# An attention and mixer kernel: the channel products' operands become scaled float16 pairs

## The chip, the core and the metric

The kernel runs on one core of a Trainium2 chip. Its engines work from queues of their own: TensorE (PE, with its weight loads shown apart as PEld), VectorE (DVE), ScalarE (ACT), GpSimd (POOL) and SyncE (SP), which issues the DMAs. The metric is the device time of one execution in microseconds (us); a kernel's time is the median of several runs. The profile is one execution recorded by the hardware.

## The reference

Eight batches, eight heads, 576 positions, 64 columns a head. Attention is masked by blocks of 64; its output, laid side by side over the heads (512 channels), goes through a mixer with four weights.

```python
scores = q @ k.T / sqrt(64), masked to block_i >= block_j
attn = softmax(scores);  x = (attn @ v), heads side by side     # per batch 576 x 512
theta = x @ w_theta
zr, zi = x * cos(theta), x * sin(theta)
y = w_tok_r @ zr + w_tok_i @ zi                                 # over positions
u = x + y
out = u + max(u @ w_ch, 0)                                      # over channels
```

## The kernel before

The work is cut into some 2570 named parts: loads, one evicting step, one group of products and so on. The order of all parts is written out by hand: the list `PLACES` (from line 32) gives each part a place, `BANKS` the bank of the matmul memory for each group, `ON` (line 185) the engine of each part that several engines could do (P, D, A for GpSimd, VectorE, ScalarE), and `RUNNING` (line 181) places at which fillers, products of ones, keep TensorE at work; there are 49 of them. Each engine's queue holds its parts in that order.

A pair is two heads of one batch; there are 32. For a pair the scores are products (L554, L567), a maximum of each row is taken on VectorE (L588), the exponentials on ScalarE (L592). For the first four pairs the exponentials are turned by TensorE (L604) and evicted by VectorE or ScalarE (`keep_half`, L611 and L613); for the others they are split into two float16 parts (`high` on ScalarE, `low` on VectorE, L619) and turned by a DMA. Products with the values (L638) and a normalising step (L653) give one tile of x per pair, kept in `x_ring`, a ring of `X_BUFS = 6` tiles.

The mixer, per batch: x is split into two float16 parts and turned; the angles are products with `wth_h` and `wth_l` (`theta`, L727), brought to turns (L737, L743) and through sine and cosine on ScalarE (L749 to L763). `times_x` (L773) makes z, in ten pieces a batch, on VectorE or GpSimd; `z_high` and `z_low` (L786) split it. The token products (`mix`, L796) take 27 products of 288 columns for each of eight results, three per block of positions: high times high, low times high, high times low. `add_parts` (L801) puts x into `u_all`, `unscale` (L805) takes the batch's scale off it, `take_u` (L809) adds the token product. For the channel products u is split into `uh` (ScalarE, L815) and `ul` (VectorE or GpSimd, L820), both 32-bit, and `channel` (L828) takes 12 products of 288 columns for each of eight results, with the 32-bit weights `wch_h` and `wch_l`. `rectify` (L834) adds the clipped result to u, and `store` (L838) writes four tiles a batch. `u_all` is one buffer of four tiles: the next batch's sums wait for the stores.

The weights come in 64-bit and are narrowed (`exponent`, `narrow`, L397 to L406). For the token and angle weights `most` (L410) sums the magnitudes, and from these a power of two is made (`w_reduce`, `w_diagonal`, `w_all`, `w_scale`) by which `high_part` (L415) and `low_part` (L421) scale them into two float16 parts. The channel weights have no scale: L417 and L424. The raw weights go in turn through two buffers that are later `uh` and `ul`.

```python
for ww, uu in ((wch_h, uh), (wch_h, ul), (wch_l, uh)):
    nc.tensor.matmul(g[:, 0:HS], lhsT=ww[:, dt, e * P:(e + 1) * P], rhs=uu[:, dt, th * HS:(th + 1) * HS],
                     start=(n == 0), stop=(n == 11))
```

Of the kernel before, what the change touches and what calls it, by code (L numbers as in the profile page):

```python
# [28 lines left out]
X_BUFS = 6  # L29
# [171 lines left out]
      "xs": "DDDDDDDDDDDDDDDD",  # L201
      "xd": "DDDDAAAAAAAAADAD",
      "uh": "AAAAAAAAAAAAAAAA",
      "ul": "DDDPDPPPPPPPDDPP"}
WHOLE = 4
PLAIN = 16

# [878 lines left out]
```

## Time and profile before

| | us |
|---|---|
| median of 3 runs | 680.8 (678.14 to 681.47) |
| profiled execution | 677.4 |
| its span, first to last instruction | 675.6 |
| TensorE busy | 658.2 (97%) |
| VectorE busy | 563.8 (83%) |
| ScalarE busy | 525.9 (78%) |
| GpSimd busy | 186.7 (28%) |
| mean granted TensorE clock | 0.997 |

A share of busy time is an average over the span. The end of a product is modelled, and products overlap, so a busy TensorE says only that one was under way; the pace of products is read from the chain, where each piece lasts until the next begins.

### The profile page before, as it was taken

Reading aid. Unit: us, or ns where it says so; the run is one execution under the profiler, and the core shown is the slowest. Engines: PE = TensorE matmul, PEld = TensorE weight load, DVE = VectorE, ACT = ScalarE, POOL = GpSimd, SP = SyncE. Lnnn points to the kernel's source line nnn. Section 1 sums busy time; section 2 is a strip of 40 time slices with the busy share of each in tenths; the row PEclk is TensorE's granted clock in tenths of the full one; section 3 lists DMA queues with packets and bytes.
Section 4 is the critical chain, followed back from the end, with each engine's and each line's share of the span. In section 5 each row is a group of like instructions: output and inputs, shape, how many; then the busy total and the mean of one; then the engine's idle time right before and its main releaser. Section 6 shows DMA issues by size and latency. Waiting matters only on the chain.

```text
span 675.6 us, 17319 instructions
## 1 busy us (share of the span) xinstructions
PE 658.2 (97%) x7263; PEld 530.9 (79%) x7263; DVE 563.8 (83%) x825; ACT 525.9 (78%) x812; POOL 186.7 (28%) x195
## 2 busy tenths in 40 slices
PE   8899999999979999999999999999999999999997
PEld 4688757889658868887798878888788887886887
DVE  4889897988988888999989888989888989864832
ACT  5999898877898699987987789878998689627410
POOL 1432222400042114241362323252054113011611
PEclk9999999999989999999999999999999999999999
DMA  9972357999969995899968896979978962960101
GB/s 337 334 257 79 106 102 137 228 214 182 244 85 229 213 197 128 182 176 207 195 176 181 165 193 147 191 131 186 203 176 181 170 131 60 172 105 1 71 1 71
DMA packets 245854, 110.51 MB, mean 164 GB/s; under 512 B 227216, under 2 KB 227216, under 8 KB 245776
## 3 DMA queue, kind: packets, MB, share of 16 engines
q1 hardware_dynamic: 245776, 109.40, 74.2%
q8 instruction: 57, 0.93, 0.6%
q14 instruction: 21, 0.17, 0.1%
HBM read 43.06 MB, written 9.44 MB: 78 GB/s over the span
## 4 chain that ended last, share of the span: by engine, by line
PE 74%; ACT 10%; DVE 8%; DMA 5%; issue 2%; POOL 0%; SPq 0%; DVEq 0%; ACTq 0%; POOLq 0%
PE ps L796 27%; PE ps L828 15%; PE ps L727 11%; PE ps L638 10%; PE ps L554 9%; DMA pt<-p 3%; ACT t L592 2%; DVE m L588 2%; DVE p L619 1%; PE ps L567 1%; DMA w_raw<-in_w_tok 1%; DMA k<-in_kT 1%; ACT aa L761 1%; DVE v L540 1%; ACT p L316 1%
## 5 line engine op out<-in xcount | busy, mean ns | idle before, releaser
L592 ACT ACTIVATE t<-ps,m 128x320 f32<-128x320 f32 (+4 forms) x320 | 149.3, 528 | 40.3 <-DVE m L588 31.7
L796 PE MATMUL ps<-wT_h,zl 128*128 128x288 f16 x540 | 155.1, 287 | 0.9 <-POOL zl L786 0.9
L796 PE MATMUL ps<-wT_h,zh 128*128 128x288 f16 x540 | 155.3, 288 | 0.4 <-ACT zh L314 0.4
L796 PE MATMUL ps<-wT_l,zh 128*128 128x288 f16 x540 | 155.0, 287 | 0.0
L588 DVE TENSOR_REDUCE m<-ps 128x2 f32<-128x128 f32 (+4 forms) x160 | 125.4, 817 | 21.9 <-PE ps L559 15.4
L796 PEld LDWEIGHTS <-zh 128*128 128x128 f16 x1080 | 106.0, 98 | 28.6 <-ACT zh L314 0.9
L638 PE MATMUL ps<-v,pt 128*128 128x65 f16 (+1 forms) x2760 | 114.5, 200 | 2.6 <-DVE x_ring L653 2.4
L619 DVE SCALAR_TENSOR_TENSOR p<-t,p 128x1664 f16<-128x1664 f32 x56 | 107.9, 1929 | 8.2 <-ACT p L316 8.0
L316 ACT ACTIVATE p<-t 128x1664 f16<-128x1664 f32 x56 | 88.8, 1591 | 6.5 <-DMA pt<-p 5.4
L638 PEld LDWEIGHTS <-pt 128*128 128x128 f16 x2520 | 82.2, 97 | 9.0 <-issue 4.8
L727 PE MATMUL ps<-wth_h,xt 128*128 128x512 f16 (+1 forms) x384 | 87.6, 345 | 0.5 <-DVE xt L713 0.3
L727 PEld LDWEIGHTS <-xt 128*128 128x128 f16 (+1 forms) x576 | 46.0, 102 | 44.3 <-issue 2.2
L828 PE MATMUL ps<-uh,wch_h 128*128 128x288 f32 x256 | 79.5, 310 | 0.0
L828 PE MATMUL ps<-ul,wch_h 128*128 128x288 f32 x256 | 75.7, 296 | 0.0
L828 PE MATMUL ps<-uh,wch_l 128*128 128x288 f32 x256 | 75.6, 295 | 0.0
L796 PEld LDWEIGHTS <-zl 128*128 128x128 f16 x540 | 53.1, 98 | 13.8 <-POOL zl L786 1.1
L727 PE MATMUL ps<-wth_l,xt 128*128 128x512 f16 (+1 forms) x192 | 57.3, 344 | 0.0
L554 PE MATMUL ps<-k,qh 64*128 64x288 f32 (+3 forms) x384 | 51.2, 400 | 2.7 <-ACT pt L611 1.5
L786 POOL TENSOR_TENSOR zl<-aa,zh 128x512 f16<-128x512 f32 (+1 forms) x27 | 33.7, 1255 | 71.1 <-ACT zh L314 71.1
L828 PEld LDWEIGHTS ps<-uh,wch_h 128*128 128x128 f32 x256 | 48.1, 188 | 2.8 <-issue 1.2
L809 DVE SCALAR_TENSOR_TENSOR u_all<-ps,sizes,u_all 128x288 f32<-128x288 f32 x64 | 31.8, 512 | 20.2 <-PE ps L796 19.2
L828 PEld LDWEIGHTS ps<-ul,wch_h 128*128 128x128 f32 x256 | 48.1, 188 | 0.3
(141 smaller groups left out, 1214.1 us busy)
## 6 DMA issues: line engine op xcount, KB each, us to landing
raw_v<-in_v SPq DMA_DIRECT2D x32, 384.0 KB, 4.3
q<-in_qT SPq DMA_DIRECT2D x32, 320.0 KB, 3.8
k<-in_kT SPq DMA_DIRECT2D x32, 320.0 KB, 3.6
out<-u_all SPq DMA_DIRECT2D x32, 288.0 KB, 2.4
w_raw<-in_w_tok SPq DMA_DIRECT2D x9, 576.0 KB, 5.8
w_raw<-in_w_theta SPq DMA_DIRECT2D x4, 512.0 KB, 7.6
w_raw<-in_w_ch SPq DMA_DIRECT2D x4, 512.0 KB, 4.9
pt<-p SPq DMA_TRANSPOSE x56, 6.4
```

Of the source, the lines that this page charges most:

```text
L316: engine.mul(to, x, scale)
L540: nc.vector.scalar_tensor_tensor(out=self.v2[:, :, :, 0:D], in0=self.v, scalar=self.batch.up, in1=self.v1[:, :, :, 0:D], op0=ALU.mult, op1 ...
L554: nc.tensor.matmul(s[hh][:, col:col + n], lhsT=qq[rows, i * P:(i + 1) * P], rhs=kk[rows, k0:k0 + n], start=nn == 0 and (j == 0 or c == "ab ...
L588: nc.vector.tensor_reduce(out=m, in_=s, axis=AX.XY if i in (2, 3) else AX.X, op=ALU.max, negate=True)
L592: nc.scalar.activation(out=to, in_=s, func=AF.Exp, scale=1.0, bias=m)
L619: nc.vector.scalar_tensor_tensor(out=self.p[:, 1, :], in0=self.t, scalar=LIFT, in1=self.p[:, 0, :], op0=ALU.mult, op1=ALU.subtract)
L638: nc.tensor.matmul(o[:, i, :], lhsT=pp[:, block, :], rhs=vv[:, of, hh, :], start=nn == 0, stop=nn == n - 1)
L727: nc.tensor.matmul(g[rows, 0:cols.stop - cols.start], lhsT=x[:, dt, part, i, rows], rhs=ww[:, dt, cols], start=(n == 0), stop=(n == 11))
L786: engine_of("zl", (2 * self.b + hf) * 5 + n).tensor_tensor(out=zl, in0=cv, in1=zh, op=ALU.subtract)
L796: nc.tensor.matmul(g, lhsT=zz[:, kk, cols], rhs=ww[:, kk, ts], start=(n == 0 and kk == k0 and nn == 0), stop=(n == 4 and nn == 2))
L809: nc.vector.scalar_tensor_tensor(out=self.u(dt)[:, ts], in0=bank("y", self.b, dt, th)[:, 0:HS], scalar=self.batch.unit, in1=self.u(dt)[:, ...
L828: nc.tensor.matmul(g[:, 0:HS], lhsT=ww[:, dt, e * P:(e + 1) * P], rhs=uu[:, dt, th * HS:(th + 1) * HS], start=(n == 0), stop=(n == 11))
```

## The change

The channel products' operands become scaled float16 pairs, as the token products' are. For that the channel weights get a sum of magnitudes and a scale of their own, and u is kept in a scaled form throughout: `unscale` multiplies x by a factor for all batches (`g_x`) in place of the batch's own, `take_u` uses `g_y`, and a new step `unlift` (parts "fin") multiplies the result by `unit` before the store, one of 576 columns a tile, two of 288 in the last batch. The factors come from `gains`, eight small steps, which need a bound on the token product: `sums_of_tok`, 18 products of ones with the magnitudes of the token weights, made before their high parts are written. `uh` is f16(u x scale), on ScalarE; `ul` is always on VectorE. Both share one buffer, `uhl`. The freed space holds `u_all` twice, for even and odd batches, and eight tiles in `x_ring`. The raw weights go in turn through `uhl` and through `p_both`, the two tiles of split exponentials now in one. `PLACES`, `BANKS`, `RUNNING` (52 fillers) and `ON` are new; in `ON`, z has 35 pieces on VectorE (46 before), its low parts 33 (30), evictions of turned exponentials 7 (5), scalings of the first values 3 (1), and "fin" has 40, of which 36 are used: 12 on GpSimd, 11 on VectorE, 13 on ScalarE.

```diff
-X_BUFS = 6
+X_BUFS = 8
-    (12, 0, 7), (24, 0, 12), (33, 0, 3), (46, 0, 4), (65, 0, 2), (75, 0, 2), (314, 0, 2), (371, 3, 10), (386, 5,
-    2), (740, 1, 5)
+    (12, 0, 7), (25, 0, 13), (43, 0, 8), (63, 0, 3), (75, 0, 3), (336, 0, 3), (396, 3, 8), (404, 5, 2), (767, 1, 5)
...
-    u_all = const.tile([P, NDT, S], F32, name="u_all")
+    u_all = [const.tile([P, NDT, S], F32, name=f"u{i}") for i in range(2)]
-    p_parts = [const.tile([P, 2, WIDE], F16, name=f"p{i}") for i in range(2)]
+    p_both = const.tile([P, 2 * 2 * WIDE], F16, name="p")
+    p_parts = [p_both.rearrange("p (h a c) -> p h a c", h=2, a=2)[:, hh] for hh in range(2)]
-    wch_h = const.tile([P, NDT, DM], F32R, name="wch_h")
-    wch_l = const.tile([P, NDT, DM], F32R, name="wch_l")
+    wch_h = const.tile([P, NDT, DM], F16, name="wch_h")
+    wch_l = const.tile([P, NDT, DM], F16, name="wch_l")
-    raws = [mo.tile([P, 2, 2 * S], U32, tag=tag, name="w_raw") for tag in ("uh", "ul")]
+    raws = [mo.tile([P, 2, 2 * S], U32, tag="uhl", name="w_raw"),
+            p_both[:, 0:8 * S].bitcast(U32).rearrange("p (k c) -> p k c", k=2)]
...
         def high_part(self):
-            if self.kind in w_up:
-                times(engine_of("w5", self.unit), self.hi, self.val, w_up[self.kind])
-            else:
-                nc.scalar.copy(out=self.hi, in_=self.val)
+            times(engine_of("w5", self.unit), self.hi, self.val, w_up[self.kind])
         def low_part(self):
-            if self.kind in w_up:
-                nc.vector.scalar_tensor_tensor(out=self.lo, in0=self.val, scalar=w_up[self.kind], in1=self.hi, op0=ALU.mult,
-                                               op1=ALU.subtract)
-            else:
-                nc.gpsimd.tensor_tensor(out=self.lo, in0=self.val, in1=self.hi.bitcast(F32), op=ALU.subtract)
+            nc.vector.scalar_tensor_tensor(out=self.lo, in0=self.val, scalar=w_up[self.kind], in1=self.hi, op0=ALU.mult,
+                                           op1=ALU.subtract)
+    def sums_of_tok():
+        g = bank("w1")
+        for th in range(2):
+            for kt in range(NK):
+                nc.tensor.matmul(g[:, th * BANK:th * BANK + HS], lhsT=ones, rhs=wT_h[:, kt, th * HS:(th + 1) * HS].bitcast(BF16),
+                                 start=kt == 0, stop=kt == NK - 1)
...
         def u_parts(self):
-            return [self.tile_of(tag, [P, NDT, S], F32R) for tag in ("uh", "ul")]
+            both = self.tile_of("uhl", [P, 2, NDT, S], F16)
+            return [both[:, i] for i in range(2)]
...
-            times(engine_of("xd", self.b * 2 + dp), u, u, self.batch.down)
+            times(engine_of("xd", self.b * 2 + dp), u, u, g_x)
...
-            engine_of("ul", self.b * 2 + dp).tensor_tensor(out=ul[:, two, ts], in0=u_all[:, two, ts], in1=uh[:, two, ts].bitcast(F32), op=ALU.subtract)
+            nc.vector.scalar_tensor_tensor(out=ul[:, two, ts], in0=u_all[self.b % 2][:, two, ts], scalar=w_down["ch"],
+                                           in1=uh[:, two, ts], op0=ALU.mult, op1=ALU.subtract)
...
+        def unlift(self, e, *th):
+            u = self.u(e)[:, th[0] * HS:(th[0] + 1) * HS] if th else self.u(e)
+            times(engine_of("fin", (self.b * NDT + e) if not th else B * NDT + 2 * e + th[0]), u, u, self.batch.unit)
...
-        if kind != "ch":
-            add(("wa", n), w.most, scaled)
-            scaled += [("wc", kind, 2)]
+        add(("wa", n), w.most, scaled)
+        scaled += [("wc", kind, 2)] + ([("wd",)] if kind == "tok" else [])
...
+    add(("wd",), sums_of_tok, [("wa", n) for n, w in enumerate(todo) if w[0] == "tok"], takes=[(("w1",), 2)])
-            free = turn_of(f"u{dp}", [("store", b, dt) for dt in two])
+            free = turn_of(f"u{dp}", [("store", b, dt) for dt in two], 2)
-            part("store", (e,), m.store, [("out", b, e, th) for th in range(2)])
+            halves = [(th,) for th in range(2)] if b == B - 1 else [()]
+            for th in halves:
+                part("fin", (e,) + th, m.unlift, [("out", b, e, i) for i in th or (0, 1)] + [("us", b, 0)])
+            part("store", (e,), m.store, [("fin", b, e) + th for th in halves])
```

## Rows read from the trace of the kernel before

**Rows 1.** Busy time of each engine, and the chain that ended last by engine.
```profile
PE 658.2 (97%) x7263; PEld 530.9 (79%) x7263; DVE 563.8 (83%) x825; ACT 525.9 (78%) x812; POOL 186.7 (28%) x195
PE 74%; ACT 10%; DVE 8%; DMA 5%; issue 2%; POOL 0%; SPq 0%; DVEq 0%; ACTq 0%; POOLq 0%
```
**Rows 2.** Stretches: start:end, length, busy us (x instructions) per engine, granted clock, DMA.
```profile
17.00:104.40 87.40, 81.23 (x714) 64.78 (x713) 77.85 (x126) 82.36 (x132) 26.89 (x37) 1.00 0.54 173
...
190.00:197.00 7.00, 3.49 (x56) 2.52 (x55) 6.41 (x11) 7.00 (x12) 5.08 (x4) 0.92 0.24 50
197.00:260.00 63.00, 63.00 (x698) 48.25 (x697) 55.62 (x77) 53.01 (x83) 11.72 (x12) 0.98 0.97 195
260.00:350.00 90.00, 89.78 (x1092) 74.50 (x1089) 84.99 (x122) 79.08 (x123) 35.53 (x30) 1.00 0.86 178
...
104.40:575.00 470.60, 466.24 (x5593) 378.74 (x5592) 422.36 (x607) 395.66 (x610) 136.31 (x124) 1.00 0.87 176
```
**Rows 3.** Chain in order of time, before 105 us: start us, us, what.
```profile
39.21 1.36 DVE m L588
...
52.91 2.66 DVE wT_l L421 x2
...
56.40 0.74 DVE pt L613
...
75.46 1.78 ACT t L592 x3
...
99.06 1.90 ACT t L592 x3
```
**Rows 4.** Chain in order of time, near 190 us.
```profile
190.60 1.05 ACT aa L761
```
**Rows 5.** Chain in order of time, from 621 us.
```profile
621.46 11.20 PE ps L828 x84
632.66 26.11 PE ps L796 x213
...
662.39 9.61 PE ps L828 x72
```
**Rows 6.** Weight loads by form: count, busy us, mean ns, idle before.
```profile
L796 PEld LDWEIGHTS <-zl 128*128 128x128 f16 x540 | 53.1, 98 | 13.8 <-POOL zl L786 1.1 <-DVE zl L786 0.4
...
L828 PEld LDWEIGHTS ps<-ul,wch_h 128*128 128x128 f32 x256 | 48.1, 188 | 0.3
```
**Rows 7.** Groups by form or line, work of the first 105 us (L534: min/median/max ns).
```profile
L421 DVE SCALAR_TENSOR_TENSOR wth_l<-w_val,size_theta,wth_h 128x1024 f16<-128x1024 f32 x2 | 2.5, 1280 | 0.0
L410 ACT ACTIVATE wth_h<-w_val 128x1024 f16<-128x1024 f32 x2 | 2.1, 1062 | 0.0
L613 DVE TENSOR_SCALAR pt<-ps 128x1024 f32<-128x1024 f32 x3 | 3.7, 1223 | 1.2 <-PE ps L604 0.7 <-ACT unused L459 0.5
L613 DVE TENSOR_SCALAR pt<-ps 128x640 f32<-128x640 f32 x2 | 1.6, 814 | 0.0
L611 ACT ACTIVATE pt<-ps 128x1024 f32<-128x1024 f32 x5 | 5.0, 1034 | 0.2
L611 ACT ACTIVATE pt<-ps 128x640 f32<-128x640 f32 x6 | 4.3, 710 | 0.0
L588 DVE TENSOR_REDUCE m<-ps 128x2 f32<-128x640 f32 x32 | 26.1, 816 | 0.6 <-PE ps L559 0.6
...
L534 DVE TENSOR_SCALAR v<-raw_v,sizes x1: 609/609/609, 30.4 to 30.4; 128x768 f32<-128x768 f32 x1
```
**Rows 8.** Low part of u, z and scaling: by line (min/median/max ns) or by form.
```profile
L820 DVE TENSOR_TENSOR ul<-u_all,uh x6: 1346/1358/2251, 126.5 to 609.8; 128x1152 fp32r<-128x1152 f32 x6
L820 POOL TENSOR_TENSOR ul<-u_all,uh 128x1152 fp32r<-128x1152 f32 x8 | 21.7, 2717 | 41.9 <-ACT uh L314 41.9
L773 DVE TENSOR_TENSOR aa<-aa,x_ring x28: 415/680/1786, 90.1 to 627.5; 128x512 f32<-128x512 f32 x18, 128x256 f32<-128x256 f32 x10
L320 DVE TENSOR_SCALAR u_all<-u_all,sizes 128x1152 f32<-128x1152 f32 x6 | 4.8, 807 | 0.1
```

More of the change, by code (lines that the diff above doesn't have):

```diff
@@ L28 @@
 QK_BUFS = 2
-X_BUFS = 6
+X_BUFS = 8
 PLACES = [
[132 rows of a table removed]
[135 rows of a table added]
 ]
 BANKS = [
[11 rows of a table removed]
[11 rows of a table added]
 ]
 RUNNING = [
-    (12, 0, 7), (24, 0, 12), (33, 0, 3), (46, 0, 4), (65, 0, 2), (75, 0, 2), (314, 0, 2), (371, 3, 10), (386, 5,
-    2), (740, 1, 5)
-]
-ON = {"w5": "AAAAAAA",
-      "wc": "PPDPDP",
-      "vc": "DPPDDDPDDDPPDDPPDDPPDDPP",
-      "qh": "APPPPAPAAAAAPAPAAAPAPAPPAAPAPAPP",
-      "vf": "PDPP",
-      "cp": "DADAADAAAADDAAAA",
-      "n0": "DDDDDDDDDAADDDDDAADADADADAAAADDDDAAADDDADDDADDDDDAAAAADAADDADDDA",
+    (12, 0, 7), (25, 0, 13), (43, 0, 8), (63, 0, 3), (75, 0, 3), (336, 0, 3), (396, 3, 8), (404, 5, 2), (767, 1, 5)
+]
+ON = {"w5": "AAAAAAAAA",
+      "wc": "PDDDPPPDP",
+      "vc": "DPDPPPPDPDDPPPDPPPPPPPDP",
+      "qh": "APPPPAPPPAPPPAAPAAAAPPPAPAAPPAAA",
+      "vf": "PDDD",
+      "cp": "DDDADDAADAAAADAA",
+      "n0": "DDADDDDDADDAAAAADDDDDDDADADAAAAAADADADDDAAADADADDADDADADDADDADDA",
       "v1": "DDDDAAAAAAAAAAAAAAAAAAAAAAAAAAAA",
       "high": "DDDDDDDDAAAAAAAAAAAAAAAAAAAAAAAAAAAAAAAAAAAAAAAAAAAAAAAAAAAAAAAA",
-      "kh": "DDDDDDDDDDDDDDDDPAAAPPPAPPPPAPPA",
+      "kh": "DDDDDDDDDDDDDDDDPPAPAPAPPAPAPPAA",
       "kl": "DDDDDDDDDDDDDDDDDDDDDDDDDDDDDDDD",
@@ L368, in attention_phase_mixer @@
             + [mo.tile([P, 1, S], F32, tag="rr", name="w_val")],
-            "ch": u_all[:, :, 0:DM]}
-    w_most = {"theta": const.tile([P, NDT // 2], F32, name="most_theta"), "tok": const.tile([P, (NK + 1) // 2], F32, name="most_tok")}
+            "ch": u_all[1][:, :, 0:DM]}
+    w_most = {"theta": const.tile([P, NDT // 2], F32, name="most_theta"), "tok": const.tile([P, (NK + 1) // 2], F32, name="most_tok"),
+              "ch": const.tile([P, NDT // 2], F32, name="most_ch")}
     w_size = {kind: const.tile([P, 5], F32, name=f"size_{kind}") for kind in w_most}
     w_up, w_down = ({kind: size[:, i:i + 1] for kind, size in w_size.items()} for i in (2, 3))
+    gain = const.tile([P, 7], F32, name="gain")
+    g_most, g_exp, g_down, g_up, g_x, g_out, g_y = (gain[:, i:i + 1] for i in range(7))
     class Weight:
@@ L439, in w_scale, with gains @@
         parts = (w_size[kind][:, i:i + 1] for i in range(4))
-        power_of_two(bank("w", kind) if step < 0 else None, *parts, step, 151.0, engine_of("wc", 3 * (kind == "tok") + step - 1) if step > 0 else None)
+        power_of_two(bank("w", kind) if step < 0 else None, *parts, step, 151.0, engine_of("wc", 3 * ("theta", "tok", "ch").index(kind) + step - 1) if step > 0 else None)
+    def sums_of_tok():
[4 more added lines that the diff above has]
+                                 start=kt == 0, stop=kt == NK - 1)
+    def gains(step):
+        one = float(1 << 23)
+        if step == 0:
+            g = bank("w1").rearrange("p (a c) -> p a c", a=2)[:, :, 0:HS]
+            nc.vector.tensor_reduce(out=g_most, in_=g, axis=AX.XY, op=ALU.max)
+        elif step == 1:
+            nc.gpsimd.tensor_scalar(out=g_most, in0=g_most, scalar1=1.02, scalar2=1.02, op0=ALU.mult, op1=ALU.add)
+        elif step == 2:
+            nc.vector.tensor_scalar(out=g_exp.bitcast(I32), in0=g_most.bitcast(I32), scalar1=23, scalar2=None,
+                                    op0=ALU.logical_shift_right)
+        elif step == 3:
+            nc.gpsimd.tensor_scalar(out=g_down.bitcast(I32), in0=g_exp.bitcast(I32), scalar1=-one, scalar2=253.0 * one, op0=ALU.mult,
+                                    op1=ALU.add)
+        elif step == 4:
+            nc.gpsimd.tensor_scalar(out=g_up.bitcast(I32), in0=g_exp.bitcast(I32), scalar1=one, scalar2=one, op0=ALU.mult,
+                                    op1=ALU.add)
+        elif step == 5:
+            nc.gpsimd.tensor_scalar(out=g_x, in0=g_down, scalar1=w_up["ch"], scalar2=1.0, op0=ALU.mult, op1=ALU.mult)
+        elif step == 6:
+            nc.gpsimd.tensor_scalar(out=g_out, in0=g_up, scalar1=w_down["ch"], scalar2=1.0, op0=ALU.mult, op1=ALU.mult)
+        else:
+            nc.gpsimd.tensor_scalar(out=g_y, in0=g_x, scalar1=w_down["tok"], scalar2=1.0, op0=ALU.mult, op1=ALU.mult)
     sizes = const.tile([P, B, 11], F32, name="sizes")
@@ L476, in unit_of @@
             if i == 0:
[L477 removed]
+                nc.gpsimd.tensor_scalar(out=self.unit, in0=self.down, scalar1=g_out, scalar2=1.0,
                                         op0=ALU.mult, op1=ALU.mult)
@@ L804, in unscale @@
             u = self.u_two(dp)
-            times(engine_of("xd", self.b * 2 + dp), u, u, self.batch.down)
+            times(engine_of("xd", self.b * 2 + dp), u, u, g_x)
         def take_u(self, dt, th):
             ts = slice(th * HS, (th + 1) * HS)
-            nc.vector.scalar_tensor_tensor(out=self.u(dt)[:, ts], in0=bank("y", self.b, dt, th)[:, 0:HS], scalar=self.batch.unit,
+            nc.vector.scalar_tensor_tensor(out=self.u(dt)[:, ts], in0=bank("y", self.b, dt, th)[:, 0:HS], scalar=g_y,
                                            in1=self.u(dt)[:, ts], op0=ALU.mult, op1=ALU.add)
@@ L814, in u_high @@
             ts, two = slice(th[0] * HS, (th[0] + 1) * HS) if th else slice(0, S), slice(2 * dp, 2 * dp + 2)
-            times(engine_of("uh", self.b * 2 + dp), self.u_parts()[0][:, two, ts], u_all[:, two, ts])
+            times(engine_of("uh", self.b * 2 + dp), self.u_parts()[0][:, two, ts], u_all[self.b % 2][:, two, ts], w_down["ch"])
         def u_low(self, dp, *th):
@@ L864, in attention_phase_mixer @@
         scaled = [("w", n, 3)]
-        if kind != "ch":
-            add(("wa", n), w.most, scaled)
-            scaled += [("wc", kind, 2)]
+        add(("wa", n), w.most, scaled)
+        scaled += [("wc", kind, 2)] + ([("wd",)] if kind == "tok" else [])
         add(("w", n, 5), w.high_part, scaled)
         add(("w", n, 6), w.low_part, [("w", n, 5)])
-    for kind in ("theta", "tok"):
+    for kind in ("theta", "tok", "ch"):
         add(("wr", kind), step_of(w_reduce, kind), [("wa", n) for n, w in enumerate(todo) if w[0] == kind])
@@ L876, in attention_phase_mixer @@
                 leaves=() if step >= 0 else [("w", kind)])
+    add(("wd",), sums_of_tok, [("wa", n) for n, w in enumerate(todo) if w[0] == "tok"], takes=[(("w1",), 2)])
+    for step in range(8):
+        needs = {0: [("wd",)], 3: [("wg", 2)], 4: [("wg", 2)], 5: [("wg", 3), ("wc", "ch", 2)], 6: [("wg", 4), ("wc", "ch", 3)],
+                 7: [("wg", 5), ("wc", "tok", 3)]}.get(step, [("wg", step - 1)])
+        add(("wg", step), step_of(gains, step), needs, leaves=[("w1",)] if step == 0 else ())
     for tag, last in (("zh", [("wm", "theta")]), ("zl", [("wm", "tok")]), ("aa", w_last["theta"]), ("rr", w_last["tok"]), ("xt0", w_last["tok"]), ("xt1", w_last["tok"]),
-                      ("uh", [("w", n, 3) for n in range(len(todo))]), ("ul", [("w", n, 3) for n in range(len(todo))])):
+                      ("uhl", [("w", n, 3) for n in range(0, len(todo), 2)]), ("p0", [("w", n, 3) for n in range(1, len(todo), 2)]),
+                      ("p1", [("w", n, 3) for n in range(1, len(todo), 2)])):
         turn_of(tag, last)
     for dp in range(NDT // 2):
-        turn_of(f"u{dp}", [w_last["ch"][dp]])
+        turn_of(f"u{dp}", [w_last["ch"][dp]], 2)
     batches = [Batch(b) for b in range(B)]
@@ L900, in attention_phase_mixer @@
         for i, kind in enumerate(("tok", "theta")):
-            add(("us", b, i), step_of(batch.unit_of, i), [("vc", b, 3), ("wc", kind, 3)])
+            add(("us", b, i), step_of(batch.unit_of, i), [("vc", b, 3), ("wg", 6) if i == 0 else ("wc", kind, 3)])
     mixers = [Mixer(b, batches[b]) for b in range(B)]
@@ L1002, in attention_phase_mixer @@
         c_all = [("c", b, e, th) for e, th in mixes]
-        u_free = turn_of("uh", c_all) + turn_of("ul", c_all)
+        u_free = turn_of("uhl", c_all)
         for dp in range(NDT // 2):
             two = (2 * dp, 2 * dp + 1)
-            free = turn_of(f"u{dp}", [("store", b, dt) for dt in two])
+            free = turn_of(f"u{dp}", [("store", b, dt) for dt in two], 2)
             part("xs", (dp,), m.add_parts, [key for dt in two for key in x_done[dt]] + free)
-            part("xd", (dp,), m.unscale, [("xs", b, dp), ("vc", b, 3)])
+            part("xd", (dp,), m.unscale, [("xs", b, dp), ("wg", 5)])
             for dt in two:
@@ L1014, in attention_phase_mixer @@
                         part("mix", (dt, th, n), m.mix, needs, takes=[("y", 2)] if n == 0 else ())
-                    part("u", (dt, th), m.take_u, [("mix", b, dt, th, 4), ("us", b, 0), ("xd", b, dp)], leaves=[("y", 2)])
+                    part("u", (dt, th), m.take_u, [("mix", b, dt, th, 4), ("wg", 7), ("xd", b, dp)], leaves=[("y", 2)])
             for th in [()] if b < B - 1 else [(0,), (1,)]:
```

20 lines of the change are left out of this document (10 added, 10 removed), and 289 rows, old and new, of tables (BANKS, PLACES).

## The prediction

> **What bounds the kernel now.** I read the busy shares first, then the chain of what ended last, then stretches, and only then single groups. TensorE is busy for 97% of the span and the chain runs over it for 74% of its length; VectorE and ScalarE follow at 83% and 78% [rows 1]. The shares are averages, so the stretches decide. From 17 to 104.4 us the token and angle weights are made ready and the first batch waits for them: ScalarE is busy 82.4 of 87.4 us and VectorE 77.9, and TensorE's 81.2 us there include fillers [rows 2]. From 75 to 101 us the chain runs on ScalarE alone [rows 3]. From 104.4 us on TensorE sets the pace: in 260 to 350 us it is busy 89.8 of 90 us, while VectorE is busy 85.0 of those 90 [rows 2]. One hole is left: from 190 to 197 us TensorE is busy only 3.5 of 7 us, because the chain there hangs on the sines of the next batch on ScalarE [rows 4], and the granted clock falls to a mean of 0.92 in that stretch and 0.98 in the next 63 us, so some of it ran at the lower of its two levels (1.2 instead of 2.4 GHz) [rows 2]. So a shorter TensorE instruction is worth its full price from about 104 us on, and added VectorE or ScalarE work costs time mainly before that.
>
> **The channel products.** All 768 keep their shape (128x128 weights, 288 columns); the operands change from 32-bit to float16. The token products have just that shape in float16. In the last 66 us the chain has both kinds back to back: 84 channel products in 11.20 us and 72 in 9.61 us, 133.4 ns each, and 213 token products in 26.11 us, 122.6 ns each [rows 5]. The gap is 10.8 ns, so 768 x 10.8 = **8.3 us** less, 1.04 us for each of eight batches. The weight loads agree: 188 ns against 98 ns [rows 6]; a load of 188 ns is longer than a product of 133 ns, and the next one begins as the last ends. I take the whole 8.3, since every batch's channel products lie after 104 us. Ends: 0 if it isn't the type that costs (a rival below), 8.3 if it is.
> [...]
>
> **Preparing the weights and the gains.** The channel weights now get what the other weights have: a sum of magnitudes (two more on ScalarE, 1.06 us each), a scale, and a scaled low part on VectorE, 2 x 1.28 us, instead of one on GpSimd [rows 7]. Two more evictions of turned exponentials go from ScalarE to VectorE in net (one of 1024 columns and one of 640: 1.22 + 0.81 us there, 1.03 + 0.71 less on ScalarE), two value scalings go from GpSimd to VectorE (0.61 each), and a reduction over 576 columns is new (about 0.75, from 0.82 for 640 columns) [rows 7]. With some five steps of one column (0.9) and what the new order puts on the other side of the first token product (about -1.4), VectorE gets 2.6 + 2.0 + 1.2 + 0.75 + 0.9 - 1.4 = **6.1 us** more before that product, and ScalarE 2.1 - 1.7 + 0.9 (smaller pieces and order) = **1.3 us**. TensorE gets 18 products of 288 columns for the sums of the token weights (18 x 122.6 ns = 2.2 us) and three fillers more (49 to 52); these run where it waits anyway. The same 59 TensorE parts as before stand ahead of the first token product in the new order, plus those sums and the channel weights' spread, so the freed space brings no work forward there. What does it cost? ScalarE's 1.3 us count in full, as the chain is on it. VectorE is idle for 9.6 us of the stretch [rows 2], so its 6.1 us may vanish; I count 0.9, the share of the chain from 17 to 104.4 us that lies on VectorE (12.9 of 87.4 us, 17 pieces between 39 and 57 us [rows 3]). Together **+2.2 us**. Ends: -1.7 (only ScalarE's relief counts) to +9.6 (1.3, 6.1 and the 2.2 of the sums one after the other; the spread of the token weights' scale stands behind these sums in TensorE's queue, and the high parts of the token weights wait for both).
>
> **Steady work moved.** The low part of u goes wholly to VectorE: 14 of about 1.36 us and 4 half ones of 0.7, against 6 of 1.36 before, +13.7 us; GpSimd loses 8 of 2.72 and 4 half ones, 27 us [rows 8]. Eleven of the z products go from VectorE to GpSimd (0.68 us each, -7.5), three more low parts of z come back (+2.1) [rows 8]. New is the last scaling of u before each store, 28 of 576 columns and 8 of 288: 11 of these on VectorE, about 0.43 and 0.25 us from 0.81 for 1152 columns [rows 8], +4.2; 13 on ScalarE (some 7 us), 12 on GpSimd. With the 6.1 above and small ones (-1.4) VectorE gains about 17.2 us, of which the 11 after the first token product fall nearly all between 104.4 and 575 us. There VectorE is busy 422.4 of 470.6 us now [rows 2]; it would be 433.4 of 464.4 (six batches' gain, 6.2, taken off), 93.3%. The stretch from 260 to 350 us shows it at 94.4% with TensorE still full [rows 2], so I cost this at nothing; if that cover is gone, see the second and fourth case. The scaling of u delays a store by one step and with it the release of that u; but u now has two copies, and the next batch fills the other. SyncE's queue holds the store behind it for that step; the loads queued there were issued earlier. In the freed space the sums of x can be written before the last batch's stores have gone, and two batches of normalised tiles fit. I cost this at 0: after 197 us TensorE has no idle time to give [rows 2]; it could only fill the hole at 190 us (third case).
>
> **The end.** After the last product there are now the rectifying step, the scaling of 288 columns on VectorE (0.25 and a handover) and the store: **+0.3 us**; ends 0.2 to 0.6. The low parts of the last batch take 0.7 us on VectorE instead of 1.4 on GpSimd, while 24 products cover them.
>
> **The sum.** -8.3 + 2.2 + 0.3 = **-5.8 us** against the profiled execution of 677.4 us (span 675.6, 1.8 us around it): 671.6. The median of the runs is 680.8, 3.4 above that execution; I carry the difference over: **675.0 us**.
>
> **The rivals.**
> Second case: VectorE and GpSimd block each other. The low part of u on VectorE takes 1.35 us at best and 2.25 at worst, and a z product 0.68 and 1.79 [rows 8]: a collision costs about 1 us. If each of the ten moved low parts meets one, VectorE has 443.4 us of work from 104.4 to 575; at no more than 94.4% busy the stretch lasts 469.7 instead of 470.6. Then -0.9 + 2.2 + 0.3 - 2.1 (batches 6 and 7) = -0.5: **680.3 us**. Against it: GpSimd's work doesn't grow, since what it gains in z products and scalings it loses in low parts.
> The page "SBUF — State Buffer" of the Trainium skill, section "Who interferes with whom", says that a VectorE instruction with two SBUF inputs contends with a GpSimd instruction that reads SBUF and that the loser waits for the whole instruction. The spread of these rows agrees with that rule.
> Third case: the freed space closes the hole. TensorE's idle 3.5 us and the lower clock (0.08 x 7 + 0.02 x 63 = 1.8 us) go, and the start costs nothing: -8.3 - 5.3 + 0.3 = -13.3: **667.5 us**. For it: two batches of normalised tiles and a second u loosen just the waits between batches. Against it: the hole's chain is on ScalarE, which gets no less to do before it, and five fillers still stand at the same point of the order.
> Fourth case, slower: VectorE's idle time doesn't shrink. If the 48.2 us that it now idles from 104.4 to 575 us are waits inside its own order, its 11 us more lengthen the stretch by 11 us and TensorE's gain there is lost: 11 + 2.2 + 0.3 - 2.1 = +11.4: **692 us**. It is slower from about 6 us of that on. Against it: the 94.4% from 260 to 350 us.
> Fifth case: the change of type gives nothing per product: 2.2 + 0.3 = +2.5: **683.3 us**. Against it: the two prices stand side by side in one stretch.
>
> **How the numbers follow.** Forecast 0.50, second case 0.17, third 0.17, fourth 0.12, fifth 0.04. A measurement of this kernel can tell about 0.5% (3.4 us) from no change. Faster: four fifths of the forecast's half (it may end 2.4 us higher), the third case, and a little of the second, 0.62. Slower: the fourth, 0.12. The same: the rest, 0.26. The range takes in half of the third case and the fifth, 666.5 to 683.5; the ends of the start-up cost, -1.7 and +9.6, would give 671.1 and 682.4 and lie in it. The forecast's own range is 671 to 679.
>
> **What would show it.** The 12 channel products of a group in 1.47 us instead of 1.60, and loads of 98 ns: the first step. The first token product at about 106.6 us: the start. TensorE full from 260 us on and VectorE at 92 to 94% there: the cover. Idle time of TensorE that VectorE ends after 260 us would show the second or fourth case; a TensorE without a hole near 190 us the third. The prediction is wrong if the channel products stay at 133 ns, if the first token product comes later than 112 us, or if VectorE's own order leaves TensorE waiting.

## The result and the profile after

| | median of runs, us (range, runs) | profiled execution | span |
|---|---|---|---|
| before | 681.27 (678.14 to 683.98, 6) | 677.4 | 675.6 |
| after | 672.46 (670.66 to 676.40, 6) | 670.9 | 669.1 |

The ratio of after to before is 0.987 [0.983, 0.991]: 8.8 us less between the medians, 6.5 us less between the profiled executions. Forecast were 675.0 and, for the profiled execution, 671.6.

Busy time of the engines in the kernel after, and its chain by engine (compare [rows 1]):
```profile
PE 649.4 (97%) x7285; PEld 501.6 (75%) x7285; DVE 575.9 (86%) x844; ACT 531.5 (79%) x829; POOL 176.4 (26%) x214
PE 62%; ACT 14%; DVE 10%; DMA 8%; issue 3%; POOL 1%; SPq 0%; ACTq 0%; DVEq 0%; POOLq 0%
```
TensorE is busy for 8.8 us less, VectorE for 12.1 more, GpSimd for 10.3 less.

Stretches of the kernel after (start:end, length, busy us and instructions of PE, PEld, DVE, ACT, POOL, granted clock, DMA; compare [rows 2]). The first token product starts at 106.3 us:
```profile
17.00:106.30 89.30, 82.56 (x731) 66.40 (x732) 83.11 (x135) 83.60 (x136) 22.22 (x44) 1.00 0.54 172
190.00:197.00 7.00, 5.39 (x90) 3.85 (x87) 6.68 (x12) 6.98 (x9) 1.16 (x1) 1.00 0.57 128
260.00:350.00 90.00, 89.72 (x1149) 71.08 (x1149) 85.27 (x121) 80.10 (x128) 38.35 (x34) 1.00 0.83 178
106.30:570.00 463.70, 458.32 (x5600) 355.23 (x5600) 430.44 (x617) 395.47 (x615) 125.15 (x130) 1.00 0.86 178
```
TensorE is still full from 260 to 350 us, with VectorE busy 94.7% of that. Over the whole steady stretch VectorE is busy 92.8%.

The chain at the end of the kernel after (start us, us, what; compare [rows 5]), and the weight loads of its channel products (compare [rows 6]):
```profile
609.90 11.76 PE ps L865 x96
...
626.84 26.46 PE ps L832 x216
653.30 11.77 PE ps L865 x96
...
665.10 0.47 DVE u L871
...
665.60 0.37 DVE u L323
```
```profile
L865 PEld LDWEIGHTS <-wch_h 128*128 128x128 f16 x512 | 48.6, 98 | 14.5 <-issue 1.3 <-DVE u L871 0.2
```
A channel product (L865) now takes 11.77 / 96 = 122.6 ns, as long as a token product (L832, 26.46 / 216 = 122.5), and its load 98 ns.

Below, the **stretch** is the time from the start of the first token product to the start of the last channel product; what lies before it is the start-up, what lies behind it to the end of the span the tail.

| profiled execution | start-up | stretch | tail |
|---|---|---|---|
| before | 104.3 | 567.4 | 3.9 |
| after | 106.3 | 558.5 | 4.4 |
| difference | +2.0 | -8.9 | +0.4 |

The three add up to the 6.5 us; the differences are taken before rounding. The experiments ask of each what made it.

The whole stretch of before, then of after (length, busy us and instructions of TensorE, granted clock, DMA), and the end of the hole of [rows 2] in the kernel before:
```profile
104.29:671.70 567.41, 563.05 (x6482) 1.00 0.78 157
106.26:664.78 558.52, 552.88 (x6482) 1.00 0.77 160
```
```profile
194.00:197.00 3.00, 2.16 (x48) 0.81 0.00 0
197.00:200.00 3.00, 3.00 (x17) 0.62 0.00 0
```
TensorE was without work for 4.4 us of the stretch before and for 5.6 us after. In the execution before, the granted clock also fell from 194 to 200 us, which took some 1.7 us (an estimate: 3 x 0.19 + 3 x 0.38); in the one after it didn't fall there. So the -8.9 us are about -8.5 of shorter products, -1.7 of clock and +1.3 of waiting.

### The profile page after: what moved, and what is told of

Same layout as the page of the kernel before. It is cut to its first block, busy times and chain, and to the rows that moved or that the text cites. A ratio compares the mean times of both kernels' runs of the same rounds, so it can differ in the third digit from the quotient of the medians.

```text
span 669.1 us, 17391 instructions
## 1 busy us (share of the span) xinstructions
PE 649.4 (97%) x7285; PEld 501.6 (75%) x7285; DVE 575.9 (86%) x844; ACT 531.5 (79%) x829; POOL 176.4 (26%) x214
## 4 chain that ended last, share of the span: by engine, by line
PE 62%; ACT 14%; DVE 10%; DMA 8%; issue 3%; POOL 1%; SPq 0%; ACTq 0%; DVEq 0%; POOLq 0%
PE ps L832 25%; PE ps L763 10%; PE ps L865 9%; PE ps L673 9%; PE ps L589 7%; DMA pt<-p 5%; DVE m L623 4%; ACT t L627 3%; ACT p L319 2%; DMA q<-in_qT 2%; DVE p L654 2%; ACT aa L797 1%; ACT zh L317 1%; DMA w_raw<-in_w_theta 1%; PE ps L602 1%
## 5 line engine op out<-in xcount | busy, mean ns | idle before, releaser
L832 PE MATMUL ps<-wT_h,zh 128*128 128x288 f16 x540 | 154.7, 286 | 1.3 <-ACT t L627 0.9
L832 PE MATMUL ps<-wT_h,zl 128*128 128x288 f16 x540 | 154.4, 286 | 1.3 <-DVE zl L822 1.1
L832 PE MATMUL ps<-wT_l,zh 128*128 128x288 f16 x540 | 154.4, 286 | 0.0
L623 DVE TENSOR_REDUCE m<-ps 128x2 f32<-128x896 f32 (+4 forms) x160 | 125.0, 816 | 14.4 <-PE ps L594 9.0
L832 PEld LDWEIGHTS <-zh 128*128 128x128 f16 x1080 | 105.5, 98 | 27.4 <-issue 0.9
L654 DVE SCALAR_TENSOR_TENSOR p<-t,p 128x1664 f16<-128x1664 f32 x56 | 105.6, 1898 | 6.2 <-ACT p L319 6.1
L865 PE MATMUL ps<-uhl,wch_h 128*128 128x288 f16 x512 | 95.3, 286 | 0.2 <-DVE u L871 0.2
L865 PE MATMUL ps<-uhl,wch_l 128*128 128x288 f16 x256 | 73.2, 286 | 0.0
L832 PEld LDWEIGHTS <-zl 128*128 128x128 f16 x540 | 52.8, 98 | 15.8 <-DVE zl L822 2.0
L865 PEld LDWEIGHTS <-wch_h 128*128 128x128 f16 x512 | 48.6, 98 | 14.5 <-issue 1.3
L809 POOL TENSOR_TENSOR aa<-aa,x_ring 128x512 f32<-128x512 f32 (+1 forms) x29 | 36.2, 1257 | 54.0 <-ACT aa L799 24.9
L589 PEld LDWEIGHTS ps<-k,qh 64*128 64x128 f32 x384 | 34.8, 189 | 16.7 <-issue 3.5
L845 DVE SCALAR_TENSOR_TENSOR u<-ps,gain,u 128x288 f32<-128x288 f32 x64 | 31.5, 511 | 17.1 <-PE ps L832 16.6
L822 POOL TENSOR_TENSOR zl<-aa,zh 128x512 f16<-128x512 f32 (+1 forms) x26 | 28.0, 1079 | 48.8 <-ACT zh L317 48.6
```

Of the source, the lines that this page charges most:

```text
L589: nc.tensor.matmul(s[hh][:, col:col + n], lhsT=qq[rows, i * P:(i + 1) * P], rhs=kk[rows, k0:k0 + n], start=nn == 0 and (j == 0 or c == "ab ...
L623: nc.vector.tensor_reduce(out=m, in_=s, axis=AX.XY if i in (2, 3) else AX.X, op=ALU.max, negate=True)
L654: nc.vector.scalar_tensor_tensor(out=self.p[:, 1, :], in0=self.t, scalar=LIFT, in1=self.p[:, 0, :], op0=ALU.mult, op1=ALU.subtract)
L809: engine_of("z", (2 * self.b + hf) * 5 + n).tensor_tensor(out=cd, in0=cd, in1=x, op=ALU.mult)
L822: engine_of("zl", (2 * self.b + hf) * 5 + n).tensor_tensor(out=zl, in0=cv, in1=zh, op=ALU.subtract)
L832: nc.tensor.matmul(g, lhsT=zz[:, kk, cols], rhs=ww[:, kk, ts], start=(n == 0 and kk == k0 and nn == 0), stop=(n == 4 and nn == 2))
```

## The experiments

The theory (A): nearly the whole gain is the shorter channel product; the freed space and the order carry little, and VectorE's added work is hidden. Rivals: (B) the freed space and the new order bring it; VectorE already holds TensorE up. All times, beside the kernel before on the same chip:

| run | median, us | ratio to before | start-up, stretch, us |
|---|---|---|---|
| e1: before, float16 channel operands | 673.7 | 0.989 [0.985, 0.993] | 106.6, 561.3 |
| e2: after, again | 672.0 | 0.986 [0.983, 0.990] | 110.1, 558.4 |
| e3: after, no last scaling | 670.2 | 0.984 [0.981, 0.988] | 105.6, 557.8 |
| e4: after, low part of u twice | 687.8 | 1.009 [1.006, 1.012] | 108.0, 573.1 |
| e5b: after, low part of u once only | 671.8 | 0.987 [0.985, 0.990] | 109.6, 557.8 |
| e6: after, operands unscaled | 672.5 | 0.990 [0.986, 0.994] | 114.9, 558.0 |
| e7: after, space unused | 737.9 | 1.086 [1.083, 1.089] | 107.1, 624.6 |
| e7b: the same, sums later | 693.1 | 1.019 [1.011, 1.027] | 106.6, 578.6 |
| e10: after, six tiles, two u | 671.8 | 0.987 [0.980, 0.994] | 113.1, 559.7 |
| e8: before, products halved | 745.2 (one run) | | 117.3, 622.2 |
| e9: e1, products halved | 674.6 (one run) | | 106.5, 562.4 |

**The type alone (e1).** The kernel before, in which only the four operands of the channel products become float16, without any scale:
```diff
-    wch_h = const.tile([P, NDT, DM], F32R, name="wch_h")
-    wch_l = const.tile([P, NDT, DM], F32R, name="wch_l")
+    wch_h = const.tile([P, NDT, DM], F16, name="wch_h")
+    wch_l = const.tile([P, NDT, DM], F16, name="wch_l")
...
-            return [self.tile_of(tag, [P, NDT, S], F32R) for tag in ("uh", "ul")]
+            return [self.tile_of(tag, [P, NDT, S], F16) for tag in ("uh", "ul")]
...
```


> The kernel before, its order, engines and buffers unchanged; only the channel products' operands (u's two parts and the channel weights' two parts) are float16, without any scale. Theory A (the type sets the price of a product, and TensorE paces the kernel after 104 us): a group of 12 takes 1.47 us instead of 1.60, and the kernel gets 8.3 us faster, a ratio of 0.988 (0.985 to 0.991). Theory B (the gain of the changed kernel comes from the new order and the freed space): under 3 us, a ratio over 0.9955. Theory C (the products run faster but the other engines then hold TensorE back in this order): 12 products in 1.47 us, but 2 to 5 us gained and waits of TensorE where there were none.

The chain at the end of e1:
```profile
619.65 10.29 PE ps L828 x84
629.94 26.09 PE ps L796 x213
...
659.34 8.83 PE ps L828 x72
```
84 products in 10.29 us are 122.5 ns, against 133.3 ns in [rows 5]. The median is 7.3 us below before, most of the whole gain, so the type is the main cause: theory A by the time, with the waits of theory C. The stretch got only 6.1 us shorter, though, not 8.3, and 1.7 of these 6.1 are the clock's, which didn't fall in the stretch of e1:
```profile
106.61:667.88 561.27, 552.57 (x6482) 1.00 0.78 159
```
The products are some 8.8 us shorter (552.57 against 563.05 less 1.7), but TensorE was without work for 8.7 us, 4.3 more than before. What it waited for between 106 and 570 us in e1 (us in total, times, longest; the largest):
```profile
PE ps L638 <- DVE x_ring L653: 2.2, 1, 2.2
PE ps L638 <- DMA pt<-p: 1.5, 1, 1.5
PE ps L828 <- DVE u_all L834: 1.0, 1, 1.0
PE ps L796 <- DVE u_all L834: 0.9, 1, 0.9
```
In the kernel before only the first of these four stood there, with the same 2.2 us. Shorter products let TensorE arrive before the attention weights' transfer and VectorE's rectifying step have ended; 3.4 us of such waits are new. In the kernel after the stretch is another 2.8 us shorter, with TensorE without work for 5.6 us: the new order, together with the freed space, takes back some 3 us of the waiting.

**The control (e2)** is the kernel after, unchanged, under the chip and conditions of e1, e3 and e4.


> The changed kernel unchanged, beside the others on the same chip, as their measure: ratio to the kernel before 0.983 to 0.991, as measured before; a profiled span of 669 to 672 us.

Its stretch is 558.4 us, within 0.1 us of the first execution. Its start-up is 3.8 us longer, and so its span, 672.9 us, lies above the 669 to 672 expected; that is taken up below.

**Without the last scaling (e3):**
```diff
-            times(engine_of("fin", (self.b * NDT + e) if not th else B * NDT + 2 * e + th[0]), u, u, self.batch.unit)
+            pass
```


> The changed kernel without the last scaling of u before the stores (left out: 36 steps on three engines, 12 us of VectorE 6, ScalarE 9, GpSimd 12 us; the output stays scaled). Theory A (these steps are covered by TensorE but for the very last): 0.4 us faster than the changed kernel, at most 1. Theory B (VectorE or GpSimd limits the steady stretch): 3 us faster or more.

The median is 1.7 us below e2, more than expected. Runs at the full clock differ less: four of e3 took 669.1 to 670.5 us, three of the kernel after (e2 among them) 670.7 to 670.9. Of the stretch 0.7 us goes (557.8), of the tail 0.4 (3.9 instead of 4.4). So about 1 us is the scaling's, the rest of the 1.7 is not to be told from the spread.

**VectorE's cover, from both sides (e4, e5b).** e4 writes the low part of u twice; e5b computes it in the first batch only, and the later batches' products read the high part in its place, so that TensorE's work stays:
```diff
-            nc.vector.scalar_tensor_tensor(out=ul[:, two, ts], in0=u_all[self.b % 2][:, two, ts], scalar=w_down["ch"],
-                                           in1=uh[:, two, ts], op0=ALU.mult, op1=ALU.subtract)
+            for _ in range(2):
+                nc.vector.scalar_tensor_tensor(out=ul[:, two, ts], in0=u_all[self.b % 2][:, two, ts], scalar=w_down["ch"],
+                                               in1=uh[:, two, ts], op0=ALU.mult, op1=ALU.subtract)
```
```diff
+            if self.b == 0:
...
-                for ww, uu in ((wch_h, uh), (wch_h, ul), (wch_l, uh)):
+                for ww, uu in ((wch_h, uh), (wch_h, ul if self.b == 0 else uh), (wch_l, uh)):
```


> The changed kernel with the low part of u written twice (18 more steps on VectorE, 14 of 1.41 us and 4 of 0.82: 23 us; VectorE's busy share from 106 to 570 us goes from 92.8% to about 97%). It asks how much cover is left. Theory A (VectorE has cover up to about 94.4%, what the kernel before showed with TensorE full): 447 to 450 us of work at 94.4% need 474 to 477 us instead of 463.7: 10 to 13 us slower than the changed kernel. Theory B (VectorE can be packed to 97% without TensorE waiting): under 2 us slower.

> The kernel after, in which the low part of u is computed for the first batch only: in the other seven batches the products that read it read the high part again, so TensorE's work is the same and VectorE has about 20 us less (14 of 1.41 us). Theory A (VectorE's added steady work is hidden behind TensorE, the prediction's cover): at most 1.5 us faster than the kernel after (672.0), so 670.5 to 672; the stretch from the first token product to the last channel product stays at 557 to 558.5 us. Theory B (VectorE already holds TensorE up in the kernel after, as the double low part, +15.8 us for 23 us of work, may suggest): 3 us or more faster, at most 669.

The steady stretch of e4, then of e5b (columns as above):
```profile
108.00:583.00 475.00, 460.70 (x5581) 355.71 (x5579) 445.86 (x629) 395.20 (x614) 125.75 (x129) 1.00 0.83 174
```
```profile
109.60:574.00 464.40, 459.46 (x5613) 356.45 (x5611) 418.50 (x610) 396.54 (x619) 126.24 (x131) 1.00 0.86 179
```
Taking 19 us of work away from VectorE (556.9 busy instead of 575.9) shortens the stretch by 0.8 us: these steps cost next to nothing in the kernel after. Adding 22 us (598.0; 18 instructions more) lengthens it by 14.6, and there VectorE is busy 445.86 of 475.0 us, 93.9%. If it can't be kept busier than that, the 430.4 us of the kernel after would need 458.4 of its 463.7, and about 5 us of VectorE work would still be free. That is an estimate from one run, and not a sharp edge: by it the other 17 of the 22 us would cost at least their full time, and 14.6 were measured. No single wait carries the 14.6 us; TensorE's waits in e4 are many and short (the largest are these):
```profile
PE ps L832 <- DVE zl L822: 2.1, 2, 1.1
PE ps L589 <- ACT t L627: 1.5, 2, 0.9
PE ps L832 <- DVE u L872: 1.3, 2, 0.9
```
So theory A holds here, and my expectation for e4 (10 to 13 us) was a little low.

**Unscaled operands (e6).** The order and buffers of after, but plain float16 copies and differences: no sums or scale for the channel weights, no 18 sums of the token weights, no gains, no last scaling.
```diff
     def w_reduce(kind):
+        if kind == "ch":
+            return
...
     def gains(step):
+        return
...
-            times(engine_of("xd", self.b * 2 + dp), u, u, g_x)
+            times(engine_of("xd", self.b * 2 + dp), u, u, self.batch.down)
...
-            nc.vector.scalar_tensor_tensor(out=ul[:, two, ts], in0=u_all[self.b % 2][:, two, ts], scalar=w_down["ch"],
-                                           in1=uh[:, two, ts], op0=ALU.mult, op1=ALU.subtract)
+            nc.vector.tensor_tensor(out=ul[:, two, ts], in0=u_all[self.b % 2][:, two, ts], in1=uh[:, two, ts], op=ALU.subtract)
...
-            times(engine_of("fin", (self.b * NDT + e) if not th else B * NDT + 2 * e + th[0]), u, u, self.batch.unit)
+            return
```


> The kernel after in order and buffers, with float16 channel operands, but without scaling them: no sums and scale for the channel weights, no 18 sums of the token weights, no gains, no last scaling of u; the high part of u is a plain copy and its low part a plain difference. Theory A (the start-up work costs about the 2.2 us of the prediction, the last scaling the 1.7 us that the run without it showed): 3 to 4 us faster than the kernel after, 668 to 669, ratio to before 0.981 to 0.983, the first token product some 2 us earlier. Theory C (the start-up's added work is hidden, ScalarE's chain gets no longer): as without the last scaling, 670.2, ratio 0.984.

It came out at neither: 672.5 us at the median, and 670.2 to 670.8 in its three runs at the full clock, the same as the kernel after. With its stretch of 558.0 and its tail of 3.9 us those three runs (spans 668.5 to 669.0) leave 106.6 to 107.1 us for the start-up, an estimate, against 106.3 in after. The profiled execution of e6 had a start-up of 114.9 us, for a reason that two other runs share (below). So, by that estimate, leaving the scaling out wins nothing before the first token product that these runs can tell, though some of the work left out stood in the chain of after (the new sums, L418, from 59.8 us and a low part, L425, at 71.5 us); and no version faster than after comes of it.

**The freed space (e7, e7b, e10).** e7 gives the new order the old space, six tiles and one u; 14 sums and scalings of x (and one z product) that would come too early are put right behind what they must wait for. e7b puts these steps 20 and 25 places behind the stores, or before their first user where that comes sooner. e10 takes only the two tiles away, and moves the one z product.
```diff
-X_BUFS = 8
+X_BUFS = 6
...
-    u_all = [const.tile([P, NDT, S], F32, name=f"u{i}") for i in range(2)]
+    u_all = [const.tile([P, NDT, S], F32, name="u0")] * 2
```


> The kernel after without use of the freed space: six normalised tiles and one u as before, and the 14 steps of sums of x that need the second u put behind the last batch's stores; everything else (type, scaling, order, banks) stays. Theory A (nearly the whole gain is the type's): at most 1 us slower than after, 672 to 673. Theory B (part of the gain is the freed space's, the prediction's third case): 3 us or more slower, 675 or above, and TensorE waits for x's sums or for normalised tiles in the trace.

> As the run without use of the freed space (six normalised tiles, one u; 737.9 us), but the sums of x for the next batch stand 20 and 25 places behind the last batch's store in the order, as they stood 8 to 59 places behind it in the kernel before, and no later than their first user. Theory A (the 66 us of that run came from putting the sums right behind the stores, where VectorE waits for the store's landing with all its other work queued behind): most of the 66 us goes, 675 to 690. Theory B (the new order needs the second u itself: its token products' evictions come too soon after the last batch's stores, wherever the sums stand): 700 us or more, with TensorE waiting on VectorE's sums and evictions.

> The kernel after with two copies of u, but six normalised tiles instead of eight; one z product of the fourth batch is put ahead of the first step that rewrites its tile, the only place at which the order of after uses the seventh and eighth tile. Theory U (of the freed space only the second u matters): within 1 us of the kernel after, 671 to 673, stretch from the first token product to the last channel product 558 to 559.5 us. Theory X (the tiles matter too, as the run with late sums, 693.1 us, had both taken away): 3 us or more slower, 675 or above, TensorE waiting for normalised tiles.

What VectorE waited for in e7:
```profile
DVE u L848 <- DMA out<-u: 32.5, 11, 5.6
```
Eleven sums of x (L848 there) stand in VectorE's queue until the last store of the previous u has landed, 3 us each time, and everything behind them stands too. That is 32.5 us at its source. TensorE is busy 670.1 us of a span of 736.0, 20.7 more than in after with as many instructions: with its waits the granted clock fell to a mean of 0.963, some 27 us less clock (an estimate from that mean and the span). With the sums later (e7b) the wait for the store is gone from VectorE's list, the clock is back at 0.994, and 45 of the 66 us are gone, but 21 remain: 693.1 us lies between what the two theories of e7b gave. With two u and six tiles (e10) the stretch is 559.7, 1.1 us above after. So the second u is what the new order stands on with the sums in either of these two places (no other place was tried), and the two tiles are worth about 1 us. Yet the old order does without either (e1, 561.3): order and space together are worth 2.8 us between e1 and after, and 3.3 between e1 and e6, neither of which has the scaling, and what of it is the space's isn't shown; e7's 66 us are the price of an order that counts on it and doesn't have it, most of it by where e7 put the sums. My theory A for e7 was wrong: I had taken "little gain from the space" to mean "little loss without it".

**Columns or loads (e8, e9).** 640 of the 768 channel products, all but the first and last of each group of 12, are split into two of 144 columns, in the kernel before (32-bit) and in e1 (float16):
```diff
+                    N = HS if n in (0, 11) else HS // 2
+                    for at in range(0, HS, N):
+                        nc.tensor.matmul(g[:, at:at + N], lhsT=ww[:, dt, e * P:(e + 1) * P],
+                                         rhs=uu[:, dt, th * HS + at:th * HS + at + N], ...
```


> The kernel before (32-bit channel operands), in which 640 of the 768 channel products are split into two of 144 columns each, same weights, same results. Theory P (the 32-bit product costs 133.4 ns because each column is slower): the pair takes the same 133 ns, 680 us, unchanged. Theory L (the 188 ns load of 32-bit weights sets the pace of these products, as 117 ns for each of the 240 32-bit products of 65 columns in the kernel before suggests: 28.2 us by 240): each half takes about 117 to 125 ns, the pair 234 to 250, so 640 x 101 to 117 = 65 to 75 us more, about 750 us.

> The kernel before with float16 channel operands, unscaled (673.7 us), and the same split of 640 channel products into halves of 144 columns. Theory P and L alike, if a float16 product goes by columns (34 ns for each of the 2520 products of 65 columns: 86.3 us by 2520): half 61 to 64 ns, pair 123 to 128, so 0 to 4 us more, 674 to 678. If a load of 98 ns held each product up: pair 196, 640 x 73 = 47 us more, 720.

The chain at the end and a row of weight loads by form, of e8 and then of e9 (L830 is the channel product; 154 are 14 whole ones and 140 halves):
```profile
675.78 17.50 PE ps L830 x154
```
```profile
L830 PEld LDWEIGHTS ps<-ul,wch_h 128*128 128x128 f32 x512 | 78.9, 191 | 0.3
```
```profile
620.33 10.46 PE ps L830 x154
```
```profile
L830 PEld LDWEIGHTS <-wch_h 128*128 128x128 f16 x960 | 72.2, 98 | 6.9 <-issue 1.5
```
A 32-bit half takes (17.50 - 14 x 0.1334) / 140 = 111.7 ns, a float16 half (10.46 - 14 x 0.1226) / 140 = 62.5 ns. Half the columns cost 84% of a whole 32-bit product and 51% of a whole float16 one. So the 32-bit price isn't one of columns (a half would be 66.7 ns): something that comes once per product, whatever its columns, holds it to 111.7 ns. Theory L says that it is the load of the weights, which the split doubled along with the products. No run lets two halves share a load, so another fixed cost of a 32-bit product isn't ruled out. The Trainium skill, page "TensorE: Matmul & The Clock Gate", section "Weight-path perf modes — Fast Weight Load (FWL) and DoubleRow", says that the fast load applies to full 128-column weights that aren't FP32. The same page of the Trainium skill, section "LDWEIGHTS (loading the stationary operand)", gives columns over 1.2 as the time of a load in ns; for 128 columns that makes 107 ns, an estimate. The 111.7 ns of e8, whose weights the trace calls f32, lie 5% above that, and the float16 halves, each with a load of its own, went at 62.5 ns, well below it. The loads' own records aren't that pace: they last 191 ns in e8 and 98 in e9, longer than the products, and so overlap. How a whole 32-bit product comes to 133.4 ns, above both 111.7 and 122.6, these runs don't show.

**Why runs of one kernel differ.** Stretches of equal make are equal within 0.1 us (after and e2), but start-ups run from 104 to 117 us. TensorE from 17 us on in the kernel after and in e10, whose start-up is the same work (length, TensorE busy, granted clock, DMA):
```profile
21.00:25.00 4.00, 2.90 (x20) 1.00 0.75 298
25.00:27.00 2.00, 1.61 (x13) 1.00 0.63 180
27.00:29.00 2.00, 1.67 (x15) 1.00 0.94 307
29.00:37.00 8.00, 8.00 (x71) 1.00 0.99 366
37.00:45.00 8.00, 7.44 (x71) 1.00 0.57 184
```
```profile
21.00:25.00 4.00, 2.53 (x20) 1.00 0.64 241
25.00:27.00 2.00, 1.61 (x13) 0.90 0.75 232
27.00:29.00 2.00, 2.00 (x12) 0.50 1.04 417
29.00:37.00 8.00, 8.00 (x40) 0.50 0.90 341
37.00:45.00 8.00, 8.00 (x45) 0.58 0.40 126
```
In e10 TensorE was busy 2.53 of 4 us from 21 us on; then the granted clock fell to its lower level, 1.2 GHz, and 40 instructions filled the 8 us in which after ran 71. The first token product came 6.8 us later. e6 shows the same fall from about 28 us on, e2 two shorter ones, near 45 and 69 us; before the second TensorE had been busy 1.27 of 2 us. The start-up, which I had read as ScalarE's, is TensorE's for longer when that happens: in e10 the chain lies on TensorE from 26.2 to 45.2 us, in after from 27.3 to 38.3. In the stretch it was the same: from 190 to 197 us TensorE was busy 3.49 of 7 us before, where the clock then fell, and 3.60 in e1, where it stayed at 1.00.

## Why the prediction was right, step by step

- **The type, -8.3 us.** Right in size: 122.6 ns and loads of 98 ns, as forecast, and some 8.5 us less work for TensorE in the stretch. That the stretch itself fell by as much, 8.9 us, is in part luck: the clock that fell in the execution before and not in that of after gave 1.7 us, and new waits took 1.3. And "I take the whole 8.3, since every batch's channel products lie after 104 us" holds only nearly, and only in the new order; alone, the type gave 6.1 us of the stretch, with those 1.7 among them (e1). The cause within the product is most likely the weight load (e8, e9), but not as the prediction read it: "the next one begins as the last ends" is wrong, since the 12 loads of a group, 188 ns each, go with its 12 products in 1.60 us and so overlap.
- **The start-up, +2.2 us.** The number came, 2.0, but by luck, as far as the runs show: by the estimate from e6, the scaling work that the sum charged there costs next to nothing, and executions of one kernel differ by up to 4 us in the start-up (after and e2). What makes the start-up of after later than the 104.3 us of before stays open. In the new order, at the full clock throughout, it was 105.6 (e3), 106.3 (after) and 106.6 us (e7b), which speaks for the order; but before is the only such run of the old order, so chance is another candidate. e1, in the old order, had 106.6 us, with the granted clock at 0.71 from 102 us on and at 0.57 from 104.
- **VectorE's steady work at nothing.** Right: 92.8% busy where 93.3% was forecast, and e5b shows that its removal gives 0.8 us. I had the added work too high, 17.2 us against 12.1. The bound that I borrowed from 260 to 350 us, 94.4%, is close to where the cover ends: e4 was 93.9% busy when it lost time.
- **The end, +0.3 us.** The tail grew by 0.4 us. Over the whole kernel the last scaling costs about 1 us (e3), so the term for it was too small by some 0.7; on VectorE its 11 instructions took 5.9 us, not 4.2.
- **From the profiled execution to the median, +3.4 us.** This is the step that failed, and most of the miss. The sum gave 671.6 for the profiled execution, and 670.9 was measured. The median of after lies 1.5 us above its own execution, that of before 3.9 above its, which was the fastest of before on record. Runs follow the granted clock: of after it was 0.991 (676.4 us) to 1.000 (670.7), of before, beside the experiments, 0.983 (690.0) to 0.999 (679.2), with none at 1.000. At the same 0.997 four runs of before took 677.8 to 679.7 us, one of e2 671.8. Why before runs lower on average isn't shown.

**The rivals.** Second case, collisions: the 14 whole low parts of u on VectorE lie close together (min/median/max ns), and none is stretched as the one of 2251 ns in [rows 8] was, which ran beside a low part of z on GpSimd:
```profile
L856 DVE SCALAR_TENSOR_TENSOR uhl<-u,size_ch,uhl x18: 811/1410/1419, 130.3 to 654.8; 128x1152 f16<-128x1152 f32 x14, 128x576 f16<-128x576 f32 x4
```
That doesn't show that such a step withstands GpSimd: in the trace of after, 16 of these 18 low parts met no GpSimd instruction at all, so the case was hardly put to the test. Single z products on VectorE (L809) still take up to 1.78 us, at a median of 0.69. What the low parts cost in all is bounded by e5b, at 0.8 us.

Third case, the hole: from 190 to 197 us TensorE was busy 5.39 of 7 us, not 3.49, and the clock stayed at 1.00, which is the 1.7 us above; but in e1, with neither the space nor the order, TensorE was busy only 3.60 of these 7 us and the clock was 1.00 from 190 to 200 us too, so the space isn't shown to be the cause, and the hole isn't closed. Fourth case: doesn't hold in after, and e4 shows what it looks like when it does. Fifth case: falls by e1.

## What to carry to other kernels

A product's price is that of its operands' type as the trace shows it side by side; before counting it in full, ask which waits a faster engine will run into: in the old order here they gave back half of it, 4.3 of 8.8 us. An engine at 93% beside a full one can still be hidden, but test the cover by doubling one of its steps: here 14.6 of 22 added microseconds showed. Before a difference of two executions is laid to the change, take out what the clock did in either: a match can hide two parts that cancel. Give a sum for the profiled execution, and carry it over to other runs only after asking what makes them differ, here above all the granted clock.

## What the runs showed of the hardware that was not expected

- Products with 32-bit operands went at 111.7 ns for 144 columns (e8) and 133.4 for 288; float16 ones at 62.5 (e9) and 122.6.
- After a lull of TensorE in the start-up (busy 2.53 of 4 us in e10) the clock was at its lower level for some 17 us, and the first token product came 6.8 us later than in another execution of the same work, in which the clock stayed at its upper level. Which of the two comes differs from run to run, in the stretch too (before and e1, near 194 us).
- A wait in VectorE's queue for the landing of a store costs more than itself: 32.5 us of such waits in e7, and 45 us less time where the waiting steps stood later (e7b), about half of it by the granted clock, whose mean was 0.963 in e7 and 0.994 in e7b.
